# Tracing a layer norm between the first matmul groups of a gated MLP, with the second x tile loaded before the weights and later chunks pinned

## The chip, the cores and the metric

The kernel runs on one core of a Trainium2 chip. The time is the device time of one launch in microseconds (us), and a kernel's figure is the median of several launches. A trace's span, from its first to its last instruction, is some 1.8 us shorter than the time of the same launch (2009.4 beside 2011.14 us for the profiled launch of before). In the prediction and the expectations, the times of landings and of clock records count from a point 0.24 us earlier than the timeline does (the load of x tiles 8 to 11 in the kernel before lands at 34.6 us there and 34.3 us on the timeline); outside of them I give the timeline's. The instructions of each engine (TensorE for matmuls, VectorE and ScalarE for elementwise work, GpSimd, and SyncE, which here only issues transfers) run in a fixed order that a scheduler writes down when the program is built. It starts from the order in which the program's lines are *traced*, and may move an instruction ahead of another. That is why it matters here when a line is traced, and not only what it computes.

## The reference

The kernel computes a block and all its gradients: a layer norm `xn` of x, an A branch (a long convolution through FFTs) and a B branch (a gated MLP), for 2048 rows, a width of 1024 and a hidden width of 3584.

```python
def _B_ref(x, W_gate, W_up, W_down):
    gate = x @ W_gate                     # einsum in the original
    up = x @ W_up
    gate = gate * (gate > 0)              # relu
    return (gate * up) @ W_down
x  = A_q
xn = _layernorm(x)
out = x + _A_ref(xn, ...) + _B_ref(xn, W_gate, W_up, W_down)
# ... and the vjp of out for every input but B_x
```

For this change it is enough that 16 tiles of 128 rows must be normalised, and that the first matmuls of the B branch need the first two of them, transposed.

## The kernel before

The rows are loaded and normalised in six chunks of 1, 1, 2, 4, 4 and 4 tiles, which I number from 0. A chunk takes two passes on ScalarE (a sum and a sum of squares), a root there, and some dozen small VectorE operations. Cuts are marked with `...`.

```python
LN_CHUNKS = (1, 1, 2, 4, 4, 4)

def layer_norm(self, xn_d, jpool, jtag, spool):
    ...
    for i, n in enumerate(self.LN_CHUNKS):
        ...
        for j in range(n):      # sums, on ScalarE
            nc.scalar.activation(out=jk[:], in_=xt[:, j, :], func=ACT.Copy, accum_out=sm[:, 0, j:j + 1])
        V.tensor_scalar(out=b(0), in0=f(0), scalar1=1.0 / D, ...)
        ...
        for j in range(n):      # x - mean on VectorE, sum of squares on ScalarE
            V.tensor_scalar(out=xt[:, j, :], ... op0=ALU.subtract)
            self.ln_act = nc.scalar.activation(out=jk[:], ... func=ACT.Square, ...)
        ...
        self.ln_act = nc.scalar.activation(out=f(4), in_=f(3), func=ACT.Sqrt)
        V.reciprocal(out=f(5), in_=f(4))
        ...
        for j in range(n):      # scale; the normalised tile also goes to memory
            V.tensor_scalar(out=xt[:, j, :], ... op0=ALU.mult)
```

The first round of the MLP's backward pass works on pairs of tiles. `gate_up` transposes two tiles on TensorE, each into a buffer of its own (one of 4 in PSUM, the memory of the pool that the matmuls write to), copies them out on VectorE, and runs a gate and an up group of 16 matmuls; `grad` runs 16 more. `gate_up` of the next pair comes ahead of `grad` of this one.

```python
def gate_up(sp):
    while len(xT) < sp + 2:
        xT.append(self.flip_xn(len(xT)))               # transposes, PSUM -> SBUF copy
    for s in (sp, sp + 1):
        ps = self.ps_tile("ps_g"); self.gemm8(ps, xT[s], wg)
        nc.scalar.activation(out=ru[s][:, 0, :], in_=ps[:], func=ACT.Relu)   # frees ps
        ...
    for s in (sp, sp + 1):
        ps = self.ps_tile("ps_u"); self.gemm8(ps, xT[s], wu)
        ht = self.e1_tile("ht")                        # pool of 3, shared with "gh" of grad
        ...                                            # mask multiply and product on VectorE
        nc.sync.dma_start(out=h_d[...], in_=ht[:])
```

The top of the program loads, then traces the whole layer norm, then the FFT tables of the A branch, and only then the MLP. The A branch is woven into the MLP's matmuls after a fixed amount of them (`A_START`).

```python
load(0)
first = [b.col_block(B_W_gate, 0, "wg")]
load(1)
first.append(b.col_block(B_W_up, 0, "wu"))
load(2); load(3)
first.append(b.row_block_T(B_W_down, 0, "wdT"))
goT = [b.load_T(g, i, "goT") for i in range(4)]
load(4); a.load_shift(); load(5)
b.layer_norm(xn_d, a.tmp, "tmp", a.sm)
with tc.issue_after(b.ln_act.ins), tc.issue_after(b.ln_dve.ins):
    a.tables()
```

## Time and profile before

| | before |
|---|---|
| time, median of 3 launches | 2009.09 us (2007.18 to 2009.27) |
| TensorE busy | 1944.6 of 2009.4 us |
| TensorE waits in the first 100 us | 32.7 us |
| start of gate groups 1, 2, 3, 4 of the first block | 24.10, 43.48, 57.84, 71.10 us |
| start of the second weight block | 84.93 us |
| start of the A branch on TensorE | 105.74 us |

Of the 65 us in which TensorE is idle, about half lie in the first 50 us; the rest is spread over the other 1950 us, where no single wait is longer than 3.6 us. So the opening is the stretch that is worth an edit. (The profiled launch took 2011.14 us and is not among the three of the first row.) The starts in the table are read from TensorE's timeline. The prediction below shows the lines of the first two; the second weight block is the row below (start, duration, both in us, engine, line, operation, and how many instructions). It is the landmark that sums up the opening, because nothing is waited for between the fourth group and it.

```profile
84.93 3.62 PE L595 MATMUL ps_g<-wg,xnT 128*128 128x512 bf16 x16
```

### The profile page before, as it was taken

How to read it: one execution, taken by the hardware profiler on the slowest of the kernel's cores; microseconds unless marked ns; L12 is line 12 of the kernel's file. 1: busy time of each engine (PE TensorE's matmuls, PEld its weight loads, DVE VectorE, ACT ScalarE, POOL GpSimd, SP SyncE). 2: the span in 40 equal slices, each digit the busy share in tenths (PEclk: the TensorE clock that was granted, in tenths of full speed). 3: DMA queues.
4: the chain of work that ended last, by engine and by line, in shares of the span. 5: the costliest groups of instructions: out<-in, count | busy, mean ns of one | idle time of the engine just before them, and what ended most of it. 6: DMA issues, size and time to landing. Idle time of an engine off the chain costs nothing.

```text
span 2009.4 us, 27247 instructions
## 1 busy us (share of the span) xinstructions
PE 1944.6 (97%) x11022; PEld 916.2 (46%) x11022; DVE 996.6 (50%) x1460; ACT 694.6 (35%) x912; POOL 16.3 (1%) x36
## 2 busy tenths in 40 slices
PE   3999999999999999999999999999999999999998
PEld 1445445444444444444454444444444444444443
DVE  5769678677677756666585650000112222233332
ACT  6455456456447428384564741111000000000000
POOL 2000000000000000000000000000000000000000
PEclk8999999999999999999999999999999999999999
DMA  9864675975674674444655259422999545544551
GB/s 269 220 162 124 157 201 150 217 189 134 156 197 125 189 210 119 130 135 133 191 159 139 81 171 300 163 93 76 213 268 226 148 115 122 127 116 121 125 127 42
DMA packets 614895, 318.32 MB, mean 158 GB/s; under 512 B 449896, under 2 KB 584048, under 8 KB 614768
## 3 DMA queue, kind: packets, MB, share of 16 engines
q1 hardware_dynamic: 613488, 312.38, 59.3%
q0 software_dynamic: 1280, 4.20, 0.6%
q8 instruction: 86, 1.41, 0.3%
q14 instruction: 41, 0.34, 0.0%
HBM read 141.36 MB, written 95.44 MB: 118 GB/s over the span
## 4 chain that ended last, share of the span: by engine, by line
PE 47%; ACT 2%; DMA 1%; SPq 1%; issue 0%; DVE 0%; DVEq 0%
PE ps_x L822 19%; PE ps_w L705 17%; PE ps_o L789 8%; PE ps L65 1%; DMA hT<-h_d 1%; ACT G L69 1%; SPq L781 0%; ACT H L69 0%; ACT K L69 0%; ACT wi L743 0%; ACT B L69 0%; SPq L758 0%; PE pst L280 0%; DVE gx L837 0%; DVE gm L834 0%
## 5 line engine op out<-in xcount | busy, mean ns | idle before, releaser
L705 PE MATMUL ps_w<-ugs,xn_nat 128*128 128x512 bf16 x1792 | 400.2, 379 | 1.1 <-DMA xn_nat<-xn_d 1.0
L595 PEld LDWEIGHTS <-xnT 128*128 128x128 bf16 x1792 | 169.7, 99 | 215.8 <-issue 23.2
L705 PEld LDWEIGHTS <-xn_nat 128*128 128x128 bf16 x1792 | 170.9, 98 | 204.2 <-issue 8.2
L595 PE MATMUL ps_g<-wg,xnT 128*128 128x512 bf16 x896 | 213.6, 387 | 15.4 <-DVE xnT L621 11.4
L705 PE MATMUL ps_d<-g_nat,hs 128*128 128x512 bf16 x896 | 208.6, 381 | 3.6 <-DMA hs<-h_d 3.6
L595 PE MATMUL ps_h<-wdT,goT 128*128 128x512 bf16 x896 | 207.4, 379 | 0.0
L595 PE MATMUL ps_u<-wu,xnT 128*128 128x512 bf16 x896 | 207.3, 379 | 0.0
L789 PE MATMUL ps_o<-wd,hT 128*128 128x512 bf16 x896 | 195.8, 381 | 5.9 <-DMA hT<-h_d 5.9
L822 PE MATMUL ps_x<-wgT,ggT 128*128 128x512 bf16 x896 | 198.6, 379 | 0.0
L822 PE MATMUL ps_x<-wuT,guT 128*128 128x512 bf16 x896 | 198.6, 379 | 0.0
L791 DVE TENSOR_TENSOR o<-ps_o,ya 128x512 bf16<-128x512 f32 x32 | 21.6, 687 | 277.4 <-PE ps_o L789 277.3
L743 ACT CAST wi<-ps_w 128x512 bf16<-128x512 f32 x112 | 65.6, 586 | 233.4 <-PE ps_w L705 230.7
L789 PEld LDWEIGHTS <-hT 128*128 128x128 bf16 x896 | 87.9, 98 | 113.6 <-DMA hT<-h_d 7.4
L824 DVE CUSTOM_DVE_ANT_0 gx<-ps_x,gy 128x512 f32<-128x512 f32 x32 | 22.1, 692 | 229.9 <-PE ps_x L822 229.9
L822 PEld LDWEIGHTS <-ggT 128*128 128x128 bf16 x896 | 87.7, 98 | 105.7
L822 PEld LDWEIGHTS <-guT 128*128 128x128 bf16 x896 | 87.7, 98 | 105.7
L664 ACT CAST gh<-ps_h 128x512 bf16<-128x512 f32 x112 | 65.5, 586 | 191.9 <-PE ps_h L595 120.8
L705 PEld LDWEIGHTS <-hs 128*128 128x128 bf16 x896 | 83.1, 98 | 100.6 <-issue 9.7
L595 PEld LDWEIGHTS <-goT 128*128 128x128 bf16 x896 | 84.1, 98 | 97.8 <-issue 6.1
L291 DVE STREAM_TRANSPOSE flp<-B 128x1024 f32<-128x1024 f32 x48 | 90.2, 1935 | 47.8 <-ACT B L69 47.6
L69 ACT CAST C<-ps 128x1024 bf16<-128x1024 f32 x96 | 96.7, 1016 | 48.4 <-PE ps L65 48.4
L652 DVE SCALAR_TENSOR_TENSOR ru<-ru,ps_u 128x512 bf16<-128x512 bf16 x112 | 76.2, 681 | 64.4 <-PE ps_u L595 52.2
(156 smaller groups left out, 1714.5 us busy)
## 6 DMA issues: line engine op xcount, KB each, us to landing
ug_d<-ru SPq DMA_DIRECT2D x112, 256.0 KB, 3.5
ugs<-ug_d SPq DMA_DIRECT2D x112, 256.0 KB, 4.4
wg<-in_B_W_gate_dram SPq DMA_DIRECT2D x56, 256.0 KB, 4.7
wu<-in_B_W_up_dram SPq DMA_DIRECT2D x56, 256.0 KB, 3.2
h_d<-ht SPq DMA_DIRECT2D x112, 128.0 KB, 2.2
hs<-h_d SPq DMA_DIRECT2D x56, 256.0 KB, 4.6
out_dram<-wi SPq DMA_DIRECT2D x56, 256.0 KB, 2.1
gt<-in_grad_out_dram SPq DMA_DIRECT2D x32, 256.0 KB, 4.0
```

The source lines that it names most:

```text
L65: self.nc.tensor.matmul(out, lhsT=lhsT, rhs=rhs, start=start, stop=stop)
L69: self.nc.scalar.copy(out=out, in_=in_)
L291: self.nc.vector.transpose(out=df[:, c0:c0 + 32, :], in_=sf[:, c0:c0 + 32, :])
L595: self.nc.tensor.matmul(ps[:], lhsT=xT[:, kt * P:(kt + 1) * P], rhs=w(kt), start=(kt == 0), stop=(kt == self.DT - 1))
L652: nc.vector.scalar_tensor_tensor(out=ru[s][:, 1, :], in0=ru[s][:, 0, :], scalar=0.0, in1=ps[:], op0=ALU.is_gt, op1=ALU.mult)
L664: nc.scalar.copy(out=gh[:], in_=ps[:])
L705: self.nc.tensor.matmul(ps[:], lhsT=lhsT(st), rhs=rhs(st), start=(st == 0), stop=(st == self.ST - 1))
L743: nc.scalar.copy(out=wo[:, d, :], in_=ps[:])
L789: nc.tensor.matmul(ps[:], lhsT=hT[:, kt, :], rhs=self.wd[:, kt, oc], start=(kt == 0), stop=(kt == self.FT - 1))
L791: nc.vector.tensor_tensor(out=o0[:, oc], in0=ps[:], in1=ya[:, oc], op=ALU.add)
L822: nc.tensor.matmul(ps[:], lhsT=T[:, kt, :], rhs=W[:, kt, oc], start=(i == 0), stop=(i == n - 1))
L824: V.tensor_tensor_reduce(out=gx[:, oc], in0=ps[:], in1=gy[:, oc], scale=1.0, scalar=0.0, op0=ALU.add, op1=ALU.add, accum_out=m[:, ob:ob + 1])
```

## The change

Its intent is to let the first matmuls go before the whole layer norm has been queued. The norm becomes a generator: the MLP asks for a chunk when it needs its tiles, and takes one chunk ahead in the first block. The load of tile 1 moves ahead of the gate weights. From chunk 3 on, the first sum of a chunk is pinned: it may not move ahead of what was traced before it on its engine. The tables are traced after the first weight block.

```diff
     def layer_norm(self, xn_d, jpool, jtag, spool):
         ...
-                nc.scalar.activation(out=jk[:], in_=xt[:, j, :], func=ACT.Copy, accum_out=sm[:, 0, j:j + 1])
+                total = nc.scalar.activation(out=jk[:], in_=xt[:, j, :], func=ACT.Copy, accum_out=sm[:, 0, j:j + 1])
+                if i >= 3 and j == 0:
+                    self.tc.keep_in_program_order(total)
         ...
             st0 += n
+            yield
         ...
                 def gate_up(sp):
                     while len(xT) < sp + 2:
+                        while len(self.xn) <= len(xT):
+                            next(ln)
                         xT.append(self.flip_xn(len(xT)))
+                    if ahead:
+                        next(ln, None)
         ...
                     yield from grad(sp)
+                if ahead:
+                    with self.tc.issue_after(self.ln_act.ins), self.tc.issue_after(self.ln_dve.ins):
+                        tables()
         ...
     load(0)
-    first = [b.col_block(B_W_gate, 0, "wg")]
     load(1)
-    first.append(b.col_block(B_W_up, 0, "wu"))
+    first = [b.col_block(B_W_gate, 0, "wg"), b.col_block(B_W_up, 0, "wu")]
         ...
-    b.layer_norm(xn_d, a.tmp, "tmp", a.sm)
-    with tc.issue_after(b.ln_act.ins), tc.issue_after(b.ln_dve.ins):
-        a.tables()
+    ln = b.layer_norm(xn_d, a.tmp, "tmp", a.sm)
```

More of the change, by code (lines that the diff above doesn't have):

```diff
@@ L503, in open_left @@
         self.ps = tc.alloc_tile_pool(name="b_ps", bufs=4, space=bass.MemoryType.PSUM)
-        self.ln_x = []
+        self.ln_x, self.xn = [], []
         self.rstd = self.per.tile([P, self.ST], F32, name="rstd")
@@ L542, in layer_norm @@
         nc, D, V = self.nc, self.D, self.nc.vector
-        self.xn = []
         st0 = 0
@@ L622, in flip_xn, with hidden @@
         return xT
-    def hidden(self, first, goT, Wg, Wu, Wd, g, xn_d, h_d, ug_d):
+    def hidden(self, first, goT, ln, tables, Wg, Wu, Wd, g, xn_d, h_d, ug_d):
         nc, HS = self.nc, self.ST // 2
@@ L635, in hidden @@
                 wg, wu, wd = first if fb + half == 0 else self.weights(Wg, Wu, Wd, fb)
-                ru = {}
+                ru, ahead = {}, fb + half == 0
                 def gate_up(sp):
                     while len(xT) < sp + 2:
+                        while len(self.xn) <= len(xT):
+                            next(ln)
                         xT.append(self.flip_xn(len(xT)))
+                    if ahead:
+                        next(ln, None)
                     for s in (sp, sp + 1):
@@ L669, in grad @@
                         self.pri.now()
-                ahead = fb + half == 0
                 if ahead:
@@ L907 @@
     load(5)
-    b.layer_norm(xn_d, a.tmp, "tmp", a.sm)
-    with tc.issue_after(b.ln_act.ins), tc.issue_after(b.ln_dve.ins):
-        a.tables()
+    ln = b.layer_norm(xn_d, a.tmp, "tmp", a.sm)
     def mlp():
-        yield 0.9, b.hidden(first, goT, B_W_gate, B_W_up, B_W_down, g, xn_d, h_d, ug_d)
+        yield 0.9, b.hidden(first, goT, ln, a.tables, B_W_gate, B_W_up, B_W_down, g, xn_d, h_d, ug_d)
         yield 1.3, b.grad_down(g, h_d, out_9)
```

## The prediction

> **What bounds the kernel now.** I read the summary first: it says which engine is the bound and how much of its idle time any reordering could win.
>
> ```profile
> PE 1944.6 (97%) x11022; PEld 916.2 (46%) x11022; DVE 996.6 (50%) x1460; ACT 694.6 (35%) x912; POOL 16.3 (1%) x36
> ...
> PE   3999999999999999999999999999999999999998
> ...
> PEclk8999999999999999999999999999999999999999
> ```
>
> TensorE is busy in 1944.6 of 2009.4 us. All its idle time is 65 us, and the slices put half of it into the first 50 us. So the second view is the list of TensorE's waits in the first 100 us:
>
> ```profile
> PE ps_g L595 <- DVE xnT L621: 11.4, 4, 6.8
> PE pst_x L619 <- DMA wu<-in_B_W_up_dram: 9.6, 1, 9.6
> PE pst_x L619 <- ACT ru L645: 6.1, 1, 6.1
> PE pst_x L619 <- DVE ln_x L577: 5.6, 1, 5.6
> ```
>
> They sum to 32.7 us. That is the ceiling of this change, 1.6% of the time. The first wait is put down to the up weights, but the layer norm of tile 0 ends there too (9.54 us). Third, the timeline of TensorE (start, duration, then what the engine waited for):
>
> ```profile
> 16.23 1.03 PE L619 MATMUL pst_x<-ident,ln_x 128*128 128x128 bf16 x8 [5.60 <-DVE ln_x L577]
> 24.10 5.67 PE L595 MATMUL ps_g<-wg,xnT 128*128 128x512 bf16 x16 [6.84 <-DVE xnT L621]
> 29.61 3.62 PE L595 MATMUL ps_u<-wu,xnT 128*128 128x512 bf16 x16
> 39.29 1.86 PE L619 MATMUL pst_x<-ident,ln_x 128*128 128x128 bf16 x16 [6.06 <-ACT ru L645]
> 43.48 6.21 PE L595 MATMUL ps_g<-wg,xnT 128*128 128x512 bf16 x16 [2.33 <-DVE xnT L621]
> 49.53 3.62 PE L595 MATMUL ps_u<-wu,xnT 128*128 128x512 bf16 x16
> ```
>
> The reader is to see that 16 matmuls take 3.62 us when the engine is warm, and 5.67 and 6.21 after a long gap; transposes take 1.86 in place of the 1.06 seen later. And ScalarE's timeline, for what held the 6.06:
>
> ```profile
> 34.40 1.06 ACT L554 ACTIVATE ln_j<-ln_x 128x1024 bf16<-128x1024 bf16 x1 [4.58 <-DMA ln_x<-in_A_q_dram]
> ...
> 38.66 1.05 ACT L645 ACTIVATE ru<-ps_g 128x512 bf16<-128x512 f32 x2
> ```
>
> The four sums of chunk 4 (tiles 8 to 11, not needed for a long time) stand ahead of the relu that frees a PSUM buffer. They wait for a load that lands at 34.6 us, so TensorE waits for it too.
>
> **What the Trainium skill says.** (1) "TensorE: Matmul & The Clock Gate", What's actually happening: the array's clock is halved after about 3.4 us of idleness and restored after about 3.4 us of work. The trace agrees: its clock records turn full at 28.5, half at 38.8 and full at 49.0 us, and the mean is 0.56 in 40 to 50 us. (2) The same page, Architectural detail, calls ScalarE and VectorE strict FIFO. The trace agrees: a ready relu stood behind a waiting activation for 6 us. (3) "DMA: Bandwidth & Descriptors", Issuing engines are not separate DMA queues: all transfers share 16 engines. Moving x tile 1 ahead of the gate weights therefore moves bytes, it makes none faster: loads before chunk 2 are the same 3 MB either way.
>
> **The change, part by part.** I compared the scheduled instruction order of both programs. TensorE's is identical, and the other engines' only differ in about their first 50 to 175 rows. So nothing after about 105 us (where the A branch enters) changes but by a shift. No work is added: this is purely when each instruction of the opening can run. I carry the durations of the trace through the new order.
>
> *Tile 1 earlier.* Now it lands at 10.2 us, eighth in line; second in line it should land at 4.5, as the load that stands second now does. But VectorE's new order still does all of chunk 2's norm before the first two copies of transposed tiles (0.64 us each), and chunk 2's load keeps its place (tenth; landed at 14.5). From there: two sums, six small operations, two squares, root, eight small ones, two scalings: 22.6 now. Only one foreign sum between squares and root goes, 0.3 us. First matmul group: 24.10 becomes **23.8**. Tile 0 itself gets about 1.1 us later (tile 1's sum and subtraction are interleaved), which nobody waits for.
>
> *The relu no longer behind the later chunks.* The new ScalarE order has both relus directly after chunk 2's root. So buffers are free when the up group ends: 23.8 + 5.5 (cold) + 3.5 = 32.75. Transposes follow at once and warm, 1.06; copies of tiles 2 and 3 start when the mask multiply of the last up group (0.68) is through, at 33.7; the second gate group starts 0.75 after that, **34.4** in place of 43.48: -9.1. The clock then stays full, so this group takes 3.46 to the next one's start in place of 6.05: **-11.7** in all.
>
> *The price: chunk 3 gets traced later.* Its tiles 4 and 5 are now needed on the next round. VectorE takes chunk 3 only after the copy of tile 3 (35.4). Sums are done by then; subtractions 4 x 0.42; four squares on ScalarE at 1.04 end at 40.6; then two relus (1.1), root, and on VectorE two mask multiplies (0.68) and two products (0.42) interleaved with eight small ones (0.2): scalings begin at 45.0. TensorE has finished its first ps_h groups at 44.8, so it waits 0.75 for tile 4. Then VectorE finishes four scalings (1.68) and does two ru products (1.35) ahead of the copies: the third gate group starts at 48.8, in place of 57.84. Gaps of 0.75 + 2.2 replace 0.34: +2.6, so **-9.1**.
>
> *Next round.* Chunk 4's norm (11 small operations, four scalings) and the ru products again stand between transposes (end 60.2) and the copies (62.2): a gap of 2.75 where 1.84 is now. Fourth gate group at 63.0 against 71.10: **-8.1**. Chunk 5 runs beside the fourth round, where no transposes wait for it; buffers free in time (by some 1 us), so the second weight block starts at 76.8 against 84.93.
>
> *Tables later.* They are now behind chunk 5. About 15 us of VectorE work (1.35, 1.22, 2.29, 1.24 us operations in the trace) and five large ScalarE ones move from 59-85 us to about 74-101, relative to TensorE some 20 us later. They then reach the A branch's entry (105.74 now, about 97.5 then): its first copy hT would end at 102.7, and TensorE would want it at 101.4. **+1.3**.
>
> Sum: -8.1 + 1.3 = -6.8; 2009.1 - 6.8 = **2002.3 us**.
>
> **Rivals.** (a) *The gain is given back at VectorE.* From 160 to 200 us it is busy 39.3 of 40 us now; a backlog carried in from the tables could hold TensorE there. For it: this margin. Against it: between 105 and 130 us it has several idle gaps of 0.5 to 2 us in which to catch up. It would make the time 2005 to 2008. (b) *The clock falls again.* The new gaps have 1.06 us of transposes in about 4 us twice (44.8 to 48.8 and 59.2 to 63.0). If the monitor counts one as idle, a group or two run at half clock, 1.7 to 3 us each time: 2004 to 2008. Against it: neither single gap reaches 3 us. (c) *The whole layer-norm wait goes.* If tiles 0 and 1 let the first matmuls start at about 15 us, up to 9 us more would be won: 1993. Against it: the copies stand behind chunk 2 in VectorE's fixed order. (d) *Chunks 3 and 4 come in time*, when ScalarE or loads turn out quicker than I reckon; the 3.5 us of new gaps would vanish: 1999.
>
> **Range and chances.** (b) and (a) push up by 2 to 5 us, (d) pulls down by 3, and the three times of before spread 2 us. Predicted 2002.3 us, 8 in 10 between 1998.5 and 2007.0. A gain over 2% would need 40 us where there are 33 to be had, so faster by over 2%: 0.01. Slower by over 2% would need a new stall in a program whose later order is the same: 0.01. Within 2%: 0.98.
>
> **What would show it.** In the profile after: first gate group near 23.8 us (right for the first step); no TensorE wait on the relu, second gate group near 34.4 and 3.6 us long; new waits of 2 to 3 us on the copies before the third and fourth gate groups; second weight block near 76.8; A branch's entry near 97.5, with a wait of about 1 us on hT. The prediction would be wrong if the first group starts near 15 us, if the clock record shows a second half-speed stretch, or if VectorE's lag shows as TensorE waits between 100 and 200 us.

## The result, and the profile after

The changed kernel takes **1999.65 us** in the median of 4 launches (1997.65 to 2001.09), beside 2009.18 us (2007.18 to 2012.94) for the kernel before on the same chip. The ratio is 0.995, with a 95% interval of 0.9932 to 0.9968. Ratios here are the mean time of one kernel's fast launches over that of the other's in the same rounds, so they are not quite the ratios of the medians that I quote. This is a gain of half a per cent: real, and well within 2%.

The summary of the profile after shows hardly a trace of it. The share of TensorE's busy time is the same 97%, and only the first slice (50 us) has changed, from 3 tenths busy to 5. Some 200 of the 11022 matmul records are missing from this trace, as the count of weight loads tells, so its busy time must not be read against that of before.

```profile
PE 1929.1 (97%) x10817; PEld 914.2 (46%) x11022; DVE 995.7 (50%) x1460; ACT 693.8 (35%) x912; POOL 15.5 (1%) x36
...
PE   5999999999999999999999999999999999999998
```

TensorE's waits in the first 110 us say more (what waited and for what, total us, times, longest). The wait on the relu is gone, and the wait on the up weights has turned into one that is put down to the small operations of the norm; it ends 0.7 us later, at 10.32 in place of 9.59 us. The waits on the copies have grown from 11.4 to 13.0 us.

```profile
PE ps_g L599 <- DVE xnT L625: 13.0, 4, 7.6
PE pst_x L623 <- DVE ln_b L565: 10.3, 1, 10.3
PE pst_x L623 <- DVE ln_x L580: 1.7, 1, 1.7
```

TensorE's timeline puts the four copies' waits in their places:

```profile
21.75 6.43 PE L599 MATMUL ps_g<-wg,xnT 128*128 128x512 bf16 x16 [7.63 <-DVE xnT L625]
28.02 3.62 PE L599 MATMUL ps_u<-wu,xnT 128*128 128x512 bf16 x16
31.47 1.06 PE L623 MATMUL pst_x<-ident,ln_x 128*128 128x128 bf16 x16
33.31 3.40 PE L599 MATMUL ps_g<-wg,xnT 128*128 128x512 bf16 x15 [0.79 <-DVE xnT L625]
...
46.76 5.31 PE L599 MATMUL ps_g<-wg,xnT 128*128 128x512 bf16 x15 [2.24 <-DVE xnT L625]
...
62.25 3.63 PE L599 MATMUL ps_g<-wg,xnT 128*128 128x512 bf16 x15 [2.38 <-DVE xnT L625]
...
76.08 3.62 PE L599 MATMUL ps_g<-wg,xnT 128*128 128x512 bf16 x16
```

The reader is to see three things. The transposes at 31.47 us follow the up group without a wait, where before they waited 6.06 us and then ran at half clock; the second gate group starts 10.2 us earlier. Two new waits, 2.24 and 2.38 us, stand ahead of the third and fourth gate groups. And the group at 46.76 us took 5.31 us in place of 3.63: the clock records of this run are at half speed from 47.9 to 51.4 us. At the second weight block 84.93 - 76.08 = 8.85 us are left of the gain, and the same 8.85 us at the A branch's first matmul (96.89 in place of 105.74 us). In the repeats below, the second weight block starts at 83.59 us (before) and at 76.44 us (after), so the gain of the opening is 7.2 to 8.9 us, depending on which two profiles are compared.

ScalarE's timeline shows why the relu's wait went. The relus of the first gate group now stand ahead of the sums of chunk 3, and those of chunk 4 do not start before 45.27 us:

```profile
28.22 0.60 ACT L653 ACTIVATE ru<-ps_g 128x512 bf16<-128x512 f32 x1 [2.24 <-PE ps_g L599]
28.71 1.05 ACT L555 ACTIVATE ln_j<-ln_x 128x1024 bf16<-128x1024 bf16 x1
```

And VectorE's timeline shows what the new wait of 2.24 us is made of. The transposes end at 44.5 us, but four scalings and two products stand ahead of the copies, with a gap of 0.29 us in which VectorE itself waits:

```profile
42.85 1.67 DVE L580 TENSOR_SCALAR ln_x<-ln_x,rstd 128x1024 bf16<-128x1024 bf16 x4
44.44 0.68 DVE L673 TENSOR_TENSOR ru<-ru,gh 128x1024 bf16<-128x1024 bf16 x1
45.41 0.69 DVE L673 TENSOR_TENSOR ru<-ru,gh 128x1024 bf16<-128x1024 bf16 x1 [0.29 <-ACT gh L672]
46.02 1.28 DVE L625 COPY xnT<-pst_x 128x1024 bf16<-128x1024 bf16 x2
```

Between this pair of profiles the spans differ by 13.5 us, not by 8.85. I compared the start of every weight load, in TensorE's order, between the two. After the opening the lead stays near 9 us to 394 us; then it moves in steps of up to 1.7 us at single waits (near 400 us on a VectorE tile of the A branch) and at half-clock stretches of 3.4 us. Two runs of the same kernel differ by such steps too: between the two profiled runs of before the differences stay within 2.6 us, and the two profiled runs of after have half-clock stretches at 502 and 717 us in one and none there in the other. So I put down to the change only the 7.2 to 8.9 us of the opening, against a difference of the medians of 9.5 us, and I leave the rest open.

### The profile page after: what moved, and what is told of

Same layout as the page of the kernel before. It is cut to its first block, busy times and chain, and to the rows that moved or that the text cites. A ratio compares the mean times of both kernels' runs of the same rounds, so it can differ in the third digit from the quotient of the medians.

```text
span 1995.9 us, 27044 instructions
## 1 busy us (share of the span) xinstructions
PE 1929.1 (97%) x10817; PEld 914.2 (46%) x11022; DVE 995.7 (50%) x1460; ACT 693.8 (35%) x912; POOL 15.5 (1%) x36
## 4 chain that ended last, share of the span: by engine, by line
PE 46%; ACT 2%; SPq 1%; DMA 1%; issue 1%; DVE 0%; DVEq 0%
PE ps_x L832 19%; PE ps_w L715 17%; PE ps_o L799 8%; PE ps L65 1%; SPq L791 1%; DMA hT<-h_d 1%; ACT G L69 1%; ACT H L69 0%; SPq L768 0%; ACT K L69 0%; ACT wi L753 0%; DMA out_dram<-wi 0%; ACT B L69 0%; PE pst L280 0%; SPq L785 0%
## 5 line engine op out<-in xcount | busy, mean ns | idle before, releaser
L715 PE MATMUL ps_w<-ugs,xn_nat 128*128 128x512 bf16 x1746 | 395.3, 379 | 3.3 <-issue 1.0
L599 PEld LDWEIGHTS <-xnT 128*128 128x128 bf16 x1792 | 169.7, 99 | 217.5 <-issue 23.8
```

Source lines behind the costliest of these rows:

```text
L599: self.nc.tensor.matmul(ps[:], lhsT=xT[:, kt * P:(kt + 1) * P], rhs=w(kt), start=(kt == 0), stop=(kt == self.DT - 1))
L715: self.nc.tensor.matmul(ps[:], lhsT=lhsT(st), rhs=rhs(st), start=(st == 0), stop=(st == self.ST - 1))
```

## The experiments

The part of the change that carries the gain was to be found first. Theory A: what TensorE waited for was that ScalarE's relu stood behind sums of a chunk that had not landed, and any order that frees it (the interleaved tracing alone) gives the gain. Theory B: the scheduler moves the sums forward again unless they are pinned. The load order is a third candidate. Two parts of the change were not tried alone: the pin without the interleaved tracing, and the later place of the tables.

**r1 and r2: both kernels again.** No edit.

> The kernel before, unchanged, for the spread of its opening. If chunk 2's landing (14.5 us in the first trace of before, 12.5 in that of after) is a matter of the load order, it lands at 14 us or later again and the first gate group starts at 24.1 +/- 0.5. If it is run-to-run variation of the transfers, it lands anywhere from 12 to 15 and the first gate group moves with it. In both cases the relu wait of about 6 us and the second gate group near 43 us come back, with a second half-speed stretch. Time ratio to before 1.000.

> The changed kernel, unchanged, for its spread. Main theory (the gain is the opening, 8 to 9 us there, later differences are variation): second weight block starts at 76 to 78 us, total 8 to 11 us under before. Whether the half-speed stretch of about 3.4 us at the third gate group (48.2 to 51.6 us in the first trace) comes back is open[...].

The kernel before took 2009.36 us, ratio 1.0006 [0.9991, 1.0021]; the changed one 1998.28 us, ratio 0.9959 [0.9946, 0.9971]. r1 gave more than a repeat. In it chunk 2 landed at 12.5 us (14.3 in the first profile), and the first gate group started 1.9 us earlier, at 22.23 us. The wait on the relu took that up. TensorE's timeline:

```profile
38.69 1.87 PE L619 MATMUL pst_x<-ident,ln_x 128*128 128x128 bf16 x16 [7.44 <-ACT ru L645]
```

The wait on the relu is longer by 1.4 us and ends at 38.69 us in place of 39.29. Its end is not set by when the group ran, but by chunk 4's landing (33.7 us here, 34.3 there) and the four sums behind it. The second weight block starts 1.34 us earlier, but 0.6 us of that came with chunk 4, and the rest with a second gate group that ran at half clock for less of its time (5.47 in place of 6.21 us). Before the pin, an earlier start of the first group is worth almost nothing.

**r3: the load order alone, on the kernel before. r4: the change without the load order.**

```diff
 # r3, against before                  # r4, against after
-    first = [... "wg"]                +    first = [... "wg"]
     load(1)                                load(1)
-    first.append(... "wu")            -    first = [... "wg", ... "wu"]
+    first = [... "wg", ... "wu"]      +    first.append(... "wu")
```

> Before with only the load order of the change (x tile 1 second in line). Main theory (the relu behind chunk 4's sums made the wait, load order is worth nothing): first gate group 22 to 24, relu wait still 5 to 7 us, second gate group 42 to 44, ratio to before 0.999 to 1.001. Rival (load order is what won): second gate group under 38 and ratio under 0.997.

> After with the load order of before. Main theory: no relu wait, second gate group at 34 to 36, ratio to before 0.994 to 0.997, like the changed kernel. Rival (load order is what won): the gain falls under 3 us, ratio over 0.9985.

r3 took 2009.14 us, ratio 1.0009 [0.9996, 1.0021]: nothing. Its relu wait is 6.65 us and its second weight block starts at 84.01 us. r4 took 2001.92 us, ratio 0.9972 [0.9959, 0.9986]: it keeps the gain in the profile (second gate group at 33.78 us, no wait on the relu, second weight block at 74.72 us, 1.4 us earlier than after, as its clock stays full in the opening), while its median is 3.6 us above that of r2 beside it. Both r4's ratio and its second gate group lie just outside what I had expected. The intervals of r2 and r4 overlap. The load order is not what brings the gain; whether it adds a little on top, these runs do not settle.

**e5: the change without the pin.**

```diff
-                if i >= 3 and j == 0:
+                if i >= 99 and j == 0:
                     self.tc.keep_in_program_order(total)
```

> After without the pin of chunks 3 to 5. In its ScalarE order the sums of chunk 3 and two of its squares stand ahead of the first relu, those of chunk 4 ahead of the second pair of relus. Theory A (interleaved tracing alone frees the first relus; the pin only postpones chunk 3 and so makes the new wait ahead of the third gate group): second gate group at 32 to 35, wait ahead of the third gate group under 1 us instead of 2.2, time 1 to 4 us under after. Theory B (the pin is what keeps the relu from waiting): a relu wait of 3 us or more returns, time 3 us or more over after.

It took 2008.21 us, ratio 0.9992 [0.9975, 1.0009]: no gain is left that the time can show, though the norm is still traced between the groups. ScalarE's timeline, then VectorE's, then TensorE's:

```profile
34.18 1.06 ACT L555 ACTIVATE ln_j<-ln_x 128x1024 bf16<-128x1024 bf16 x1 [5.15 <-DMA ln_x<-in_A_q_dram]
...
35.23 0.19 ACT L568 ACTIVATE ln_s<-ln_s 128x4 f32<-128x4 f32 x1
```

```profile
35.45 0.18 DVE L569 RECIPROCAL ln_s<-ln_s 128x4 f32<-128x4 f32 x1 [5.71 <-ACT ln_s L568]
```

```profile
38.27 5.50 PE L599 MATMUL ps_g<-wg,xnT 128*128 128x512 bf16 x15 [6.63 <-DVE ht L662]
...
81.53 3.62 PE L599 MATMUL ps_g<-wg,xnT 128*128 128x512 bf16 x16
```

The reader follows the wait from engine to engine. One sum of chunk 4 was moved ahead of chunk 3's root (0.19 us), which all the same stood behind it for 5.15 us; VectorE's reciprocal waited 5.71 us for the root; the copies of tiles 2 and 3 stood behind the reciprocal; and TensorE waited for the copies. (The line names `ht` and 6.63 us; one of the group's 16 records is missing. If it is the first, the group began 0.2 us earlier, right behind the copy.) Theory A falls: freeing the relu is not enough, and the relus are free here (28.45 us). Theory B stands in that the scheduler moves sums forward, though not by the sign that I had named for it: no wait on the relu came back, the wait moved to chunk 3's root. The pin, on the order that the tracing lays down, carries most of the gain, but not all of it: the second weight block starts at 81.53 us, 2.1 to 3.4 us ahead of the two profiles of before, and by the starts of the weight loads e5's lead over the first of them is still 3.2 us at the end. The interval of its ratio is too wide to tell 3 us from nothing.

**e6: is it the landing?** The kernel before, with chunk 4 loaded ahead of `wdT` and `goT`, so that the sums that stand in the way have their data.

```diff
     load(3)
+    load(4)
     first.append(b.row_block_T(B_W_down, 0, "wdT"))
     goT = [b.load_T(g, i, "goT") for i in range(4)]
-    load(4)
```

> Before with one change: chunk 4 of x (1 MB) is loaded ahead of the down weights and the gradients. ScalarE's order stays. Main theory (what the relu waited for in before is chunk 4's landing at 34.6 us): chunk 4 lands before 25, the relu wait of 6.1 us falls under 2.5, second gate group at 38 to 40 and at full clock, ratio to before 0.996 to 0.998. Rival (the norm's work on ScalarE and VectorE is the bound of the opening, not the load): second gate group stays at 42 to 44, ratio 0.999 or more.

Chunk 4 landed at 19.1 us, and the wait on the relu went, though on ScalarE the four sums of chunk 4 still stand ahead of the relus (TensorE's timeline):

```profile
34.80 1.06 PE L619 MATMUL pst_x<-ident,ln_x 128*128 128x128 bf16 x16
37.31 3.40 PE L595 MATMUL ps_g<-wg,xnT 128*128 128x512 bf16 x15 [1.46 <-DVE xnT L621]
```

So the landing was the cause, reached from the other side. But it took 2005.83 us, ratio 0.9984 [0.9967, 1.0001], and its second weight block starts at 80.25 us: the first group is later (25.29 us), as the scheduler here put the copies of tiles 0 and 1 behind chunk 3's subtractions on VectorE, and the fourth gate group waits 3.97 us, after which the clock is at half speed for 3.4 us. The ratio missed the expected 0.996 to 0.998. By the profile, loading earlier is a weaker cure than the pin; the intervals of the ratios of e6 and r2 just overlap.

**e7: the rest of the first wait.** In the changed kernel the copies of tiles 0 and 1 still stand behind chunk 2's norm, which holds the first group till 21.75 us. Here chunk 2's first VectorE operation is pinned as well.

```diff
-            V.tensor_scalar(out=b(0), in0=f(0), scalar1=1.0 / D, ...)
+            mean = V.tensor_scalar(out=b(0), in0=f(0), scalar1=1.0 / D, ...)
+            if i == 2:
+                self.tc.keep_in_program_order(mean)
```

> After with chunk 2's first VectorE instruction pinned behind the copies of transposed tiles 0 and 1. Main theory (the 7.6 us wait ahead of the first gate group is VectorE's order, its data being ready): first gate group at 13.5 to 15 instead of 21.8 to 23.8, all later groups move with it, time 5 to 9 us under after (about 1991 to 1995). Rival (transfers take over: chunk 2, down weights, gradients or chunk 4 not there yet): first gate group moves, but 4 us or more come back as waits before the second weight block, time under 3 us below after.

The first group started at 13.95 us, 7.8 us earlier, and the second at 24.72. Yet the kernel took 2002.43 us, ratio 0.9964 [0.9947, 0.9981], no better than after. The rival's count came true, though not for its reason, late loads. TensorE's timeline, then VectorE's:

```profile
13.95 5.64 PE L601 MATMUL ps_g<-wg,xnT 128*128 128x512 bf16 x16
...
40.11 1.89 PE L625 MATMUL pst_x<-ident,ln_x 128*128 128x128 bf16 x16 [5.08 <-DVE ln_x L582]
45.45 0.61 PE L601 MATMUL ps_g<-wg,xnT 128*128 128x512 bf16 x1 [3.46 <-DVE xnT L627]
...
74.70 3.62 PE L601 MATMUL ps_g<-wg,xnT 128*128 128x512 bf16 x16
```

```profile
38.21 0.42 DVE L664 TENSOR_TENSOR ht<-ru 128x512 bf16<-128x512 bf16 x1 [5.27 <-DMA h_d<-ht]
```

VectorE waited 5.27 us for a *store*: `ht` and `gh` share three buffers, and the fourth product needs one that an h_d store has not yet read out. SyncE's queue says why. The first product had been done at 22.5 us, but its store was issued at 32.15 us, behind four transposing loads of `goT`, two x chunks and the next gate weights:

```profile
19.08 6.32 SPq L618 DMA_TRANSPOSE goT<-in_grad_out_dram  x4
...
27.96 4.08 SPq L594 DMA_DIRECT2D wg<-in_B_W_gate_dram  x3
32.15 0.41 SPq L665 DMA_DIRECT2D h_d<-ht  x1
```

**s1 and s4: those eight stores on another queue,** with e7's pin (s1) and without it (s4).

```diff
-                        nc.sync.dma_start(out=h_d[...], in_=ht[:])
+                        q = nc.gpsimd if ahead else nc.sync
+                        q.dma_start(out=h_d[...], in_=ht[:])
```

> The copies-first version (first gate group at 14 us, whose 8 us came back as a wait on a product that waited for an h_d store) with the eight h_d stores of the first weight block issued from GpSimd's queue instead of SyncE's, where they stood behind loads. Main theory (the 5.1 and 3.5 us waits ahead of the third gate group came from h_d stores standing in SyncE's queue while they held the three shared buffers): both waits together fall under 4 us, second weight block starts at 67 to 71 us instead of 74.7. Then the tables on VectorE should be the next bound: 2 to 6 us of waits at the A branch's entry. Time 1996 to 2001. Rival (transfers themselves too slow, or GpSimd's stores queue behind its own xn stores): the waits stay over 6 us and the time at 2002.

> The changed kernel with only the first block's eight h_d stores issued from GpSimd's queue, chunk 2's norm left where it stands. Theory (the stores hold buffers only where the first group is made to start early): in the changed kernel no instruction of the opening waits for an h_d store, so nothing is won: second weight block at 75.5 to 77 us, ratio 0.995 to 0.997, like the changed kernel. Rival (the stores' queue alone brings what the version with both gained): second block at 73 us or earlier, ratio at or below 0.9945.

s1 issued its first store at 23.18 us, and TensorE's timeline reads:

```profile
40.21 6.59 PE L601 MATMUL ps_g<-wg,xnT 128*128 128x512 bf16 x16 [3.90 <-DVE xnT L627]
...
70.81 3.62 PE L601 MATMUL ps_g<-wg,xnT 128*128 128x512 bf16 x16
```

It took **1997.05 us** (1994.39 to 1999.94, 6 launches), ratio 0.9945 [0.9928, 0.9961], the lowest median of all versions. The second weight block starts 3.9 us before e7's and 5.3 us before the changed kernel's. A cost is left: the third group waits 3.90 us and runs at half clock. Half of this wait is a store once more. ScalarE's timeline, then VectorE's:

```profile
38.24 0.58 ACT L675 CAST gh<-ps_h 128x512 bf16<-128x512 f32 x1 [3.93 <-DMA h_d<-ht]
```

```profile
38.86 0.69 DVE L676 TENSOR_TENSOR ru<-ru,gh 128x1024 bf16<-128x1024 bf16 x1 [1.95 <-ACT gh L675]
```

So the other queue has shortened the waits for the three buffers and not removed them; a pool of more than three was not tried. The waits at the A branch's entry that I had expected at 2 to 6 us came to 1.8. The interval of s1 overlaps with those of the changed kernel (0.995 and 0.9959), and the two were not timed in the same rounds, so that it beats the changed kernel is likely but not shown.

s4 took 2000.60 us, ratio 0.9963 [0.9949, 0.9976]: as the theory had it in the ratio, but its second block, at 77.14 us, is just outside the expected range, and the premise was wrong. I had written that nothing in the changed kernel's opening waits for an h_d store. ScalarE does: its copy to `gh` waits 1.90 us for one there, which is where VectorE's gap of 0.29 us came from. Over GpSimd's queue that wait is longer (ScalarE's timeline of s4), and VectorE's gap behind it 1.06 us:

```profile
45.85 0.59 ACT L673 CAST gh<-ps_h 128x512 bf16<-128x512 f32 x1 [3.04 <-DMA h_d<-ht]
```

The view of the transfers has the reason: a store of 128 KB took 2.8 us from issue to landing over SyncE's queue in the changed kernel and 4.5 us over GpSimd's in s4. So in these profiles the other queue gains where SyncE's is blocked (e7) and loses a little where it is not; in the ratios s4 and the changed kernel are the same.

**e8: smaller chunks, against the two new waits.** Chunk 3 (tiles 4 to 7) is cut into halves, so that only two tiles' scalings stand ahead of the copies. The second half is loaded after the gradients, and each later chunk moves on by one round, so that the last one is traced after the fourth round, ahead of the tables.

```diff
-    LN_CHUNKS = (1, 1, 2, 4, 4, 4)
+    LN_CHUNKS = (1, 1, 2, 2, 2, 4, 4)
...
+                    for _ in ln:
+                        pass
                     with self.tc.issue_after(self.ln_act.ins), ...:
                         tables()
...
     load(5)
+    load(6)
```

> After with the chunk of tiles 4 to 7 cut into two chunks of 2. Main theory (the waits of 2.2 and 2.4 us ahead of the third and fourth gate groups are VectorE's work on whole chunks of 4 between the transposes and the copies): the wait ahead of the third gate group falls under 1.5 us and time 1 to 4 us under after. Rival (the waits are set by the ru products and relus, not the chunk's size; the halves add 11 small operations): waits as before, time same or up to 2 us over after.

The two waits fell to 0.34 us each, no half-clock stretch came between the first group and 100 us, and the second weight block started at 69.29 us, 6.8 us before the changed kernel's. The time was 2001.39 us, ratio 0.9958 [0.994, 0.9977]: the same, where I had expected 1 to 4 us less. Counted by the weight loads, the lead over the changed kernel is 5.5 us where the A branch enters, and 40 us later e8 is 2.2 us behind. TensorE's timeline at the A branch's entry has what took it back, a wait on the first VectorE copy of that branch, followed by half clock from 110.7 to 117.5 us:

```profile
111.40 1.04 PE L65 MATMUL ps<-hT,R 64*128 64x512 bf16 x4 [3.87 <-DVE hT L77]
```

That copy starts at 110.12 us, 11 us later than in the changed kernel (99.09), and not because VectorE was busy all that time. It stood still for 4.90 us on a `gh` copy that itself waited for an h_d store, and for 3.47 us on the sums of the last chunk. ScalarE's timeline, then VectorE's:

```profile
85.49 0.59 ACT L672 CAST gh<-ps_h 128x512 bf16<-128x512 f32 x1 [5.12 <-DMA h_d<-ht]
```

```profile
86.11 0.69 DVE L673 TENSOR_TENSOR ru<-ru,gh 128x1024 bf16<-128x1024 bf16 x1 [4.90 <-ACT gh L672]
```

How much of the 11 us is the stores and how much the later place of the last chunk, no run here separates.

**s2 and s3: start the A branch later,** which was to give VectorE time for the tables. s2 is e8 with `A_START` at 64_000 in place of 55_000; s3 has everything: e7's pin, GpSimd's stores, e8's chunks and `A_START` at 76_000.

> The halves version (second weight block at 69.3 us, but a 3.9 us wait on hT and a half-speed stretch at the A branch's entry) with the A branch entering about 6 matmul groups later. Main theory (VectorE's tables and last norm were not done when TensorE wanted hT, so the opening's gain was given back): wait on hT under 0.5 us, no half-speed stretch near 110 us, time 3 to 7 us under the halves version, 1994 to 1998. Rival (a backlog of VectorE is only moved, and TensorE waits for it later, in the A branch's first stretch): time within 2 us of 2001.

> Copies first, h_d stores of the first block from GpSimd, halves, and the A branch about 13 groups later. If the three waits are independent and all of them are the order of instructions: first gate group at 14, second weight block at 61 to 65, time 1986 to 1993. If transfers become the bound (gradients, chunk 4, up and down weights of block 2 arrive on SyncE's single queue): second weight block or its ps_h groups wait for loads, 3 us or more, and the time is 1992 to 1997.

Both failed, and the times lie outside what any of the theories and rivals gave. s2 took 2011.47 us, ratio 1.002 [1.0005, 1.0034]; its wait on `hT` is still 3.64 us. s3 took 2018.49 us, ratio 1.0056 [1.0039, 1.0073], slower than before although its second weight block starts at 66.05 us. After that TensorE waits on VectorE: 12.4 us in total on the tiles `ru` and 10.4 us on the A branch's `flp`, with 5.2 and 5.9 us as the longest, and the A branch ends at 1228.0 us, beside 1195.4 us in e8 (1211.6 in s2). The branch gained nothing from the later start. A mere backlog of VectorE does not explain it: from 70 to 160 us VectorE is busy 63.2 of 90 us in s3 and 74.7 in the changed kernel. The `gh` copies on ScalarE wait 27.4 us for h_d stores between 60 and 160 us in s3 (4.6 us in the changed kernel), one of them 10.98 us, so the three shared buffers may be the bound here too. That was not tested. Why the ends come later by so much I have not found out: I did not vary `A_START` alone on the changed kernel, nor the place of the tables alone.

## Why the prediction was right or wrong

The time was predicted as 2002.3 us, in a range of 1998.5 to 2007.0; it is 1999.65 and, in the second batch, 1998.28 us. It lay within 2%, and the mechanism that carries the gain held. Of the sum's two terms, the -8.1 us for the opening came out at -8.85 by the first pair of profiles and at -7.15 by the repeats, and the +1.3 us for the tables at nothing. The first pair would account for 2.05 of the 2.65 us between 2002.3 and 1999.65, but the opening's gain itself differs by 1.7 us between the pairs. That the opening's sum came so close is partly luck: the third gate group was 2.04 us ahead of the step, and a stretch of half clock that the sum had left out gave 1.7 us of that back. By its own steps:

- **First gate group, 23.8 us.** Measured 21.75 and, in r2, 22.70. The order of VectorE was right (the copies stand behind chunk 2's norm), and rival (c), which would have it near 15 us, did not come. The step took chunk 2's landing in before, 14.3 us on the timeline, as fixed; it was 12.3 and 13.2 us, and 12.5 in the repeat of before, so the same kernel spreads by 1.8 us, and r1 shows that before the change this is worth almost nothing. The step also miscounted the queue: x tile 1 stood sixth and chunk 2 eleventh, behind 2.5 MB; nothing in the sum hangs on it.
- **The relu no longer behind chunk 4; second gate group at 34.4 us, warm.** Measured 33.31 (r2: 33.74), with a full clock. This is the step that carries the gain, and e6 shows its cause. What the step did not say is that the pin does it: it read the finished order, in which tracing and pin cannot be told apart, and e5 shows that the tracing alone leaves 2.1 to 3.4 us of the gain in the profile and none that the time can show.
- **New waits of 0.75 and 2.2 us, third group at 48.8 us.** One wait of 2.24 (r2: 1.96), third group at 46.76 us (47.12). The 0.75 did not come. Of the 2.04 us by which the third group beat the step, 1.1 us were inherited from the second. Most of the rest comes, as I read it, from adding up VectorE's operations end to end, where in the timeline an operation often starts up to 0.1 us before the recorded end of the one before. The scalings began at 42.85 us and not at 45.0; 1.5 of these 2.15 us are the earlier start of chunk 3 on VectorE (33.88 in place of 35.4 us). And 0.29 us of the wait is a cause that the step did not have, a `gh` copy that waited for a store (see s4).
- **The clock then stays full.** Wrong for the third group: it ran at half clock from 47.9 to 51.4 us, and likewise in the second profile of the changed kernel, which cost 5.31 - 3.63 = 1.7 us. The prediction had named such a stretch as a sign that it is wrong; of its three signs this one came. This is rival (b), which I gave "1.7 to 3 us each time" and argued against because "neither single gap reaches 3 us". It came once, not at the fourth group, where the gap was longer (2.38 us).
- **Fourth group 63.0, second weight block 76.8 us.** Measured 62.25 and 76.08 (r2: 62.62 and 76.44). The wait of 2.38 us ahead of the fourth was put at 2.75. The opening was thus worth 8.85 us, where the sum had 8.1.
- **Tables later, +1.3 us at the A branch's entry.** This term failed. VectorE's timeline and TensorE's show `hT` done at 100.32 us and taken at 100.81 without a wait:

```profile
99.09 1.23 DVE L77 COPY hT<-pst 128x2048 bf16<-128x2048 bf16 x1
```

```profile
100.81 0.39 PE L65 MATMUL ps<-hT,R 64*128 64x512 bf16 x2
```

  The step put the end of that copy at 102.7 us, 2.4 us too late; I take the cause to be the same, durations added end to end, but did not check it. The direction was not idle: the margin is 0.5 us, and in s4 the same matmul waits 0.38 us.
- **Rival (a), the gain given back at VectorE,** did not come in the changed kernel, whose lead is 8.85 us at the entry as at the second weight block, and whose TensorE waits for nothing on VectorE from 100 to 200 us. In e8, s2 and s3 a gain was given back at VectorE, though in e8 and s3 VectorE itself waited for stores. **Rival (d)** did not come: both new waits are there.

## What to carry to other kernels

An instruction that waits for a load holds everything behind it on its engine, and an engine's order is the scheduler's, not the source's; look in the timeline for a short ready operation behind a long wait, and pin the one that waits, since moving the lines alone may be undone (here the changed kernel took 2008.21 us without the pin, and 1999.65 us with it). Before you shorten a wait, find out what sets its end: an earlier start of the first group was worth almost nothing while the relu behind chunk 4 ended the wait. And when an opening has been shortened, see who is next: here it was buffers held by stores queued behind loads, and then a VectorE copy at the entry of the other branch, late in part because of such a store, and what it cost took back all of a further 7 us.

## What the Trainium skill lacked or had wrong

- "TensorE: Matmul & The Clock Gate", Why this matters for your kernels, asks for no idle gaps over about 3 us. In both profiles of the changed kernel the clock fell to half for 3.4 us behind gaps of only 2.24 and 1.96 us (with 1.06 us of transposes just ahead), and did not fall behind a gap of 2.38 us 15 us later, nor behind one of 1.87 us in r4. The clock records in these traces, but for the last of each, have lengths that are multiples of 3.413 us (the half-speed ones one to four of them), which goes with the free-running window of that page (What's actually happening); what share of a window must be idle, the page does not say and these runs do not settle.
- "DMA: Bandwidth & Descriptors", Issuing engines are not separate DMA queues, says that issuing from several engines saves only the issuing time, "usually small relative to the DMA itself". Here eight stores that no longer stood behind loads in SyncE's queue (issued at 23.18 us in place of 32.15) brought the second weight block from 74.70 to 70.81 us. What is missing is that a queue's order can hold on-chip buffers.
- The same page (Specifications) puts the first byte of a transfer issued by GpSimd some 0.4 us behind that of one issued by SyncE. Under the load of this opening the median landing of a 128 KB store was 1.7 us later (4.5 us in s4 in place of 2.8 us in the changed kernel).
- No page of it that I read gives the spread of landings between launches. Chunk 2, the eleventh transfer of its queue, landed at 14.3 and 12.5 us in the two profiled runs of before, and between 12.3 and 14.3 us in all fourteen profiled runs.
